# Attention and gated feed-forward layer: six one-bank PSUM tiles in place of three two-bank tiles

## The chip, the cores and the metric

The kernel runs on one core of one Trainium2 chip. The core has five engines, each with its own instruction stream: TensorE (PE; its weight loads are listed as PEld), VectorE (DVE), ScalarE (ACT), GpSimd (POOL) and SyncE (SP), which issues the DMAs here. Matmul results go to PSUM, an accumulator memory that this kernel uses in banks of 512 float32 values per partition. Engines wait for one another through semaphores. The metric is the time of one execution on the device in microseconds (us).

## The reference

```python
def _attn_ref(q, k, v, n_sink, window):            # B 4, H 8, S 768, D 64
    scores = (1.0 / np.sqrt(D)) * np.matmul(q, k.transpose(0, 1, 3, 2))
    pos = np.arange(S)
    rel = pos[:, None] - pos[None, :]
    keep = (pos[None, :] < n_sink) | ((rel >= 0) & (rel < window))   # 4 and 128
    scores = np.where(keep, scores, -1e9)
    a = np.exp(scores - scores.max(-1, keepdims=True))
    a = a / (a.sum(-1, keepdims=True) + 1e-9)
    return np.matmul(a, v)

def reference(...):
    x = attn_out.transpose(0, 2, 1, 3).reshape(B * S, H * D)          # 3072 x 512
    h = x @ w_in                                                      # 512 x 2048
    g = h - np.tanh(h)
    return (g @ w_out).astype(np.float32)                             # 2048 x 512
```

## The kernel before, in words

The 3072 rows of x are cut into 12 chunks of 256 (NCHUNK). Attention works in units of one chunk and one pair of heads, 48 in all; each unit has two blocks of 128 queries (t = 0, 1). The feed-forward part works in steps of one chunk (cc) and one of 8 weight groups (g) of 256 hidden columns, 96 in all. To keep float32 accuracy, operands are split into a high and a low part and multiplied in several passes.

**A unit.** `scores` multiplies a query block with a window of keys (L504 with raw operands for the first 12 units, L511 with split ones later); the two heads' results go to the two banks of one PSUM tile. `merge` works on that tile on VectorE: where `kind > 0`, L525 copies the earlier window's scores into the places that the later one leaves free, for both heads in one instruction, and then, head by head, L531 applies the mask and takes the row's extreme (an instruction and a short read of its accumulator). ScalarE takes the exponential (L539), VectorE the reciprocal of the sums (L559, L560), ScalarE scales (L565). `turn` transposes the probabilities into tbank (L599); from there ScalarE copies (L606, L616) and VectorE copies under a mask (L613). `attend` transposes the four sink columns into xbank (L640), ScalarE copies them out once per head of a pair (zr, L647), and L656 and L662 multiply with the values into xbank; ScalarE rounds the result (xh, L674) and VectorE takes the rest (xl, L678).

**A step.** L777 makes h in one of two h banks; ScalarE takes tanh (L796), VectorE the difference (L799), ScalarE the high part (L802), VectorE the low part (L805). The second product goes to an output bank by L847; from chunk 5 on (SA) a seven-product scheme is used instead (L881), whose sums lie in sbank and obank, with more vector work in the gate (L812, L815, L818). At the end of such a chunk `gather` takes the sums out: ScalarE copies the first bank of sbank (L920), VectorE adds the second bank of obank (L924), the second of sbank (L927, L929) and the first of obank (L933).

**Which bank holds what.** PSUM has eight banks, two for h and six in three tiles of two banks each:

```python
248  sbank = ps.tile([P, 2, 512], F32, tag="s", name="sbank")
249  obank = ps.tile([P, 2, 512], F32, tag="o", name="obank")
250  txbank = ps.tile([P, 2, 512], F32, tag="tx", name="txbank")
251  tbank, xbank = txbank[:, 0, :], txbank[:, 1, :]
```

Scores go to sbank up to chunk 5 and to txbank behind it; in the first units the second block goes to obank.

**What sets the order.** Nothing is issued as the loops run. Every piece of work is handed to `Work.add` with its engine, an estimated duration, a due time and what it reads and writes; here the six banks are six names (s0, s1, o0, o1, t, x). `Work.order` (L194 to L230) plays the estimates through and gives one list, by which each engine's instructions are recorded. The due times come from a few constants (L274 to L277): PACE is the time of a step, LEAD how far attention runs ahead of the steps that need it, HALF2 how far the second product follows the first, SPILL and STREAM the due times of two kinds of DMA. Behind this list, the layer that records the program puts in the semaphore waits; it knows tiles.

**Stages.** The steps of chunks 0 to 2 are interleaved while the weights are still coming in, are decoded to high and low parts on the chip, and are written to a scratch memory (spill, `wscr`). From step 24 on, the first weights are read back from there through a ring of five blocks (`ring`, `spare`); the place in SBUF that comes free takes sums of weights for the seven-product scheme (L985, L987, L989 on `wide`, then L1001 to L1008).

## Time and profile before

| what | value |
|---|---|
| median of 3 runs | 714.76 us (714.32 to 716.55) |
| profiled execution | 713.8 us |
| its span in the trace | 712.0 us |
| mean granted TensorE clock | 0.993 of full speed |
| busy: PE, PEld | 666.9 us, 611.2 us |
| busy: DVE, ACT, POOL | 551.4, 410.0, 177.2 us |
| DMA | 137.23 MB, HBM 191 GB/s over the span |

The rows come from the profiled execution alone. A busy time counts when at least one instruction of the engine ran; "[1.00 <-DVE wide L929]" says that the engine stood idle for 1.00 us before this instruction and that VectorE's L929, which writes `wide`, was what ended the wait. Such releasers are inferred. Matmuls of one line are drawn together as x4 and the like.

### The profile page before, as it was taken

Reading aid. Unit: us, or ns where it says so; the run is one execution under the profiler, and the core shown is the slowest. Engines: PE = TensorE matmul, PEld = TensorE weight load, DVE = VectorE, ACT = ScalarE, POOL = GpSimd, SP = SyncE. Lnnn points to the kernel's source line nnn. Section 1 sums busy time; section 2 is a strip of 40 time slices with the busy share of each in tenths; the row PEclk is TensorE's granted clock in tenths of the full one; section 3 lists DMA queues with packets and bytes.
Section 4 is the critical chain, followed back from the end, with each engine's and each line's share of the span. In section 5 each row is a group of like instructions: output and inputs, shape, how many; then the busy total and the mean of one; then the engine's idle time right before and its main releaser. Section 6 shows DMA issues by size and latency. Waiting matters only on the chain.

```text
span 712.0 us, 14370 instructions
## 1 busy us (share of the span) xinstructions
PE 666.9 (94%) x5099; PEld 611.2 (86%) x5099; DVE 551.4 (77%) x1305; ACT 410.0 (58%) x1056; POOL 177.2 (25%) x287
## 2 busy tenths in 40 slices
PE   6788999999999997999999999999999998999896
PEld 5556899889988787889889889999999998999895
DVE  6777998964878898889878768877886876875554
ACT  5876333345876675656567557566565665663231
POOL 5332100001436464313222212223111231210000
PEclk9999999999999998999999999999999999999999
DMA  6769972432148665657857865866775775664761
GB/s 187 244 198 335 351 293 104 152 115 86 53 116 242 187 194 155 194 161 232 229 178 200 258 185 174 239 211 190 232 220 185 210 239 167 180 184 135 237 192 65
DMA packets 77485, 137.23 MB, mean 193 GB/s; under 512 B 8156, under 2 KB 28764, under 8 KB 77404
## 3 DMA queue, kind: packets, MB, share of 16 engines
q1 hardware_dynamic: 77404, 136.22, 62.0%
q8 instruction: 42, 0.69, 0.4%
q14 instruction: 39, 0.32, 0.1%
HBM read 120.98 MB, written 15.20 MB: 191 GB/s over the span
## 4 chain that ended last, share of the span: by engine, by line
PE 71%; DVE 10%; DMA 7%; ACT 6%; issue 2%; POOL 1%; SPq 0%; ACTq 0%; DVEq 0%
PE h L777 30%; PE sbank L881 10%; PE obank L881 7%; DMA ring<-wscr 6%; PE txbank L662 5%; PE obank L847 5%; PE txbank L847 3%; PE sbank L847 3%; PE txbank L511 3%; PE txbank L599 2%; DVE pt L613 2%; PE sbank L511 1%; ACT p L565 1%; PE txbank L656 1%; ACT pt L616 1%
## 5 line engine op out<-in xcount | busy, mean ns | idle before, releaser
L777 PE MATMUL h<-xh,ring 128*128 128x256 f32 x924 | 185.8, 282 | 8.6 <-DMA ring<-wscr 5.5
L777 PEld LDWEIGHTS h<-xh,ring 128*128 128x128 f32 x924 | 151.3, 190 | 10.9 <-DMA ring<-wscr 7.0
L777 PE MATMUL h<-xl,ring 128*128 128x256 f32 x462 | 129.0, 279 | 0.0
L796 ACT ACTIVATE gbuf<-h 128x512 f32<-128x512 f32 x96 | 57.3, 597 | 105.5 <-PE h L777 65.8
L482 POOL TENSOR_TENSOR q<-qraw,q 128x512 fp32r<-128x512 f32 x36 | 47.4, 1318 | 254.5 <-ACT q L479 254.5
L777 PEld LDWEIGHTS h<-xl,ring 128*128 128x128 f32 x462 | 87.6, 190 | 0.4
L539 ACT ACTIVATE p<-p,st 128x132 f32<-128x132 f32 x168 | 66.5, 398 | 26.8 <-DVE st L531 25.6
L815 ACT CAST ghbuf<-gbuf 128x896 fp32r<-128x896 f32 x55 | 51.9, 943 | 39.1 <-DVE gbuf L812 38.7
L777 PE MATMUL h<-xh,w 128*128 128x256 f32 x384 | 73.4, 281 | 0.0
L818 DVE TENSOR_TENSOR glbuf<-gbuf,ghbuf 128x896 fp32r<-128x896 f32 x55 | 61.2, 1112 | 15.2 <-ACT ghbuf L815 13.6
L777 PEld LDWEIGHTS h<-xh,w 128*128 128x128 f32 x384 | 60.8, 188 | 1.3 <-PE txbank L662 0.2
L565 ACT ACTIVATE p<-p,st 128x132 f32<-128x132 f32 x168 | 54.2, 394 | 4.3 <-DVE st L560 3.8
L474 DVE TENSOR_TENSOR ks<-kraw,ks 64x392 fp32r<-64x392 f32 x72 | 49.5, 687 | 5.6 <-ACT ks L469 3.0
L777 PE MATMUL h<-xl,w 128*128 128x256 f32 x192 | 53.5, 279 | 0.0
L847 PE MATMUL obank<-w,ghbuf 128*128 128x512 f32 x192 | 51.5, 399 | 1.4 <-ACT ghbuf L802 1.4
L799 DVE TENSOR_TENSOR gbuf<-h,gbuf 128x512 f32<-128x512 f32 x55 | 37.9, 689 | 18.8 <-ACT gbuf L796 18.3
L777 PE MATMUL h<-xh,spare 128*128 128x256 f32 x228 | 50.7, 285 | 0.2 <-DMA spare<-wscr 0.2
L619 POOL TENSOR_TENSOR pt<-pt,after 128x512 f32<-128x512 f32 x32 | 43.4, 1358 | 29.4 <-ACT pt L616 27.3
L613 DVE TENSOR_TENSOR pt<-txbank,below 128x512 f32<-128x512 f32 (+1 forms) x48 | 28.9, 602 | 26.8 <-ACT pt L616 9.7
L574 POOL CAST z<-p 128x16 fp32r<-128x16 f32 x42 | 11.5, 274 | 124.4 <-ACT p L565 119.2
L662 PE MATMUL txbank<-pt,v 128*64 128x128 f32 (+1 forms) x512 | 41.5, 315 | 0.0
L662 PEld LDWEIGHTS txbank<-pt,v 128*64 128x64 f32 x512 | 31.0, 137 | 11.8 <-issue 4.6
(157 smaller groups left out, 1620.8 us busy)
## 6 DMA issues: line engine op xcount, KB each, us to landing
ring<-wscr SPq DMA_DIRECT2D x231, 256.0 KB, 4.1
spare<-wscr SPq DMA_DIRECT2D x57, 256.0 KB, 4.1
qraw<-qd SPq DMA_DIRECT2D x36, 256.0 KB, 4.6
wraw<-w_in SPq DMA_DIRECT2D x16, 512.0 KB, 8.2
wraw<-w_out SPq DMA_DIRECT2D x16, 512.0 KB, 8.2
wscr<-w SPq DMA_DIRECT2D x16, 512.0 KB, 4.9
kraw<-kp SPq DMA_DIRECT2D x38, 196.0 KB, 3.9
v<-vp SPq DMA_DIRECT2D x27, 256.0 KB, 2.9
```

What stands on the lines that cost most here:

```text
L474: (nc.gpsimd if KP else nc.vector).tensor_tensor(k[o, h, :], t[r, :], k[r, h, :].bitcast(F32), op=ALU.subtract)
L482: (nc.gpsimd if QP else nc.vector).tensor_tensor(ql[u], qt[u], qh[u].bitcast(F32), op=ALU.subtract)
L539: nc.scalar.activation(e, e, AF.Exp, bias=st[u][:, j : j + 1], scale=-1.0, accum_out=st[u][:, 4 + j : 5 + j],)
L565: nc.scalar.activation(pr[u][:, j, :], pr[u][:, j, :], AF.Copy, scale=s[:, 8 + j : 9 + j])
L619: nc.gpsimd.tensor_tensor(w[:, :, 0, :], w[:, :, 0, :], after.unsqueeze(1).to_broadcast([P, 4, P]), op=ALU.mult)
L662: nc.tensor.matmul(xps[key][(p - p0) // 2][h * 64 : h * 64 + 64, p % 2, a:z], lhsT=vt[cc, i][:, hd : hd + D], rhs=rhs, start=False, stop=p ...
L777: nc.tensor.matmul(hps[n][:, f, :], lhsT=w, rhs=x, start=r == 0, stop=r == 11)
L796: nc.scalar.activation(g0, h(), AF.Tanh)
L815: nc.scalar.copy(ghbuf[:, n % 2], gbuf[:, 1:, :])
L818: nc.vector.tensor_tensor(glbuf[:, :7, :], gbuf[:, 1:, :], ghbuf[:, n % 2].bitcast(F32), op=ALU.subtract)
L847: nc.tensor.matmul(sums_of(n, cc, t), lhsT=a[:, f, t * P : (t + 1) * P], rhs=wt[1, g][:, (0, 1, 0)[i], f, :], start=first and not low and ...
L881: nc.tensor.matmul(acc, lhsT=a[:, b, :], rhs=factor(g, m, part % 2), start=g == 0 and part == 0 and m in (4, 1, 2, 7), stop=closes(n) and ...
```

## The change

Each of the six banks becomes a tile of its own; sbank, obank and txbank become pairs of tiles. Since an instruction can no longer span the two heads' banks, the masked merge L525 is issued for each head by itself, right ahead of that head's mask instruction. Of 80 such merges 160 become. Five constants of the planner have other values. The change shortens the file by five lines: L525 is L524 in the new kernel, L531 L526, L613 L608, L777 L772, L799 L794, L805 L800, L881 L876. TensorE and ScalarE keep their instructions (5516 and 1080 in the program), VectorE has 1819 in place of 1739.

```diff
-        sbank = ps.tile([P, 2, 512], F32, tag="s", name="sbank")
-        obank = ps.tile([P, 2, 512], F32, tag="o", name="obank")
-        txbank = ps.tile([P, 2, 512], F32, tag="tx", name="txbank")
-        tbank, xbank = txbank[:, 0, :], txbank[:, 1, :]
+        banks = {n: ps.tile([P, 512], F32, tag=n, name=n) for n in ("s0", "s1", "o0", "o1", "t", "x")}
+        sbank, obank, txbank = ((banks[a], banks[b]) for a, b in (("s0", "s1"), ("o0", "o1"), ("t", "x")))
+        tbank, xbank = txbank
...
-        FIRST, EARLY, PACE, LEAD = 45000.0, 4600.0, 7980.0, 43356.0
+        FIRST, EARLY, PACE, LEAD = 45000.0, 4600.0, 7956.0, 43418.0
         UNIT, SECOND, WLEAD, WNEXT = 2000.0, 3000.0, 6000.0, 2500.0
-        HALF2, LAST = 8253.0, 6188.0
-        SPILL, STREAM, DEAR, DLATE = 36773.0, 5446.0, 120000.0, 17426.0
+        HALF2, LAST = 9148.0, 6188.0
+        SPILL, STREAM, DEAR, DLATE = 47526.0, 10850.0, 120000.0, 17426.0
...
                 both = obank if apart else sbank if cc <= SA else txbank
-                ps = [both[:, h, :] for h in range(2)]
-                sps[u, t] = both, ps
+                ps = sps[u, t] = both
...
-                both, ps = sps[u, t]
+                ps = sps[u, t]
...
-                if kind > 0:
-                    nc.vector.copy_predicated(
-                        both[:, :, TS:WIN], above.bitcast(U32).unsqueeze(1).to_broadcast([P, 2, P]),
-                        both[:, :, :P],
-                    )
                 for h in range(2):
+                    if kind > 0:
+                        nc.vector.copy_predicated(ps[h][:, TS:WIN], above.bitcast(U32), ps[h][:, :P])
                     j = 2 * h + t
                     nc.vector.tensor_tensor_reduce(
...
-            4: (sbank[:, 0, :HALF], 1), 3: (sbank[:, 0, HALF:], 0), 1: (obank[:, 1, :HALF], 2),
+            4: (sbank[0][:, :HALF], 1), 3: (sbank[0][:, HALF:], 0), 1: (obank[1][:, :HALF], 2),
```

The other lines of the diff only write `bank[:, i, ...]` as `bank[i][:, ...]`.

The merges of the first units on VectorE (p and st are the probabilities and sums of one unit) before:

```order
L525 COPY_PREDICATED obank<-above,obank 128x2x128 [waits PE_49]
L531 ISA p_292,st_293<-obank,mask 128x132 [waits DVE_49]
L531 ISA st_293 128x1
L531 ISA p_292,st_293<-obank,mask 128x132
L531 ISA st_293 128x1
```

And now, where o_238 and o_239 are the two banks of obank:

```order
L524 COPY_PREDICATED o_238<-above,o_238 128x128 [waits PE_49]
L526 ISA p_296,st_297<-o_238,mask 128x132 [waits DVE_49]
L526 ISA st_297 128x1
L524 COPY_PREDICATED o_239<-above,o_239 128x128 [waits PE_49]
L526 ISA p_296,st_297<-o_239,mask 128x132 [waits DVE_49]
L526 ISA st_297 128x1
```

One merge over both heads has become two, each ahead of its head's mask, and each mask waits for its own merge.

TensorE at the end of chunk 5, where the first L881 of the next chunk follow (edge and w_0 are weights of the seven-product scheme, ghbuf the high part of the gate) before:

```order
L881 MATMUL sbank<-edge_2480,ghbuf 128x256 [waits DVE_49,Activation_49]
L881 MATMUL sbank<-edge_2480,ghbuf 128x256 x3
L881 MATMUL obank<-edge_2480,ghbuf 128x256 x2
L777 MATMUL h_4463<-xh_4114,spare 128x256 [waits DMAHW3_49,PE_49]
L777 MATMUL h_4463<-xl_4115,spare 128x256
L777 MATMUL h_4463<-xh_4114,spare 128x256 x2
L777 MATMUL h_4463<-xl_4115,spare 128x256
L777 MATMUL h_4463<-xh_4114,spare 128x256
L881 MATMUL sbank<-w_0_764,ghbuf 128x256 x4
```

And now, with s_236 and s_237 the banks of sbank and o_239 the second bank of obank:

```order
L876 MATMUL s_236<-edge_2502,ghbuf 128x256 [waits Activation_49]
L876 MATMUL s_236<-edge_2502,ghbuf 128x256 x3
L876 MATMUL o_239<-edge_2502,ghbuf 128x256 [waits DVE_49]
L876 MATMUL o_239<-edge_2502,ghbuf 128x256
L772 MATMUL h_4514<-xh_4161,spare 128x256 [waits DMAHW3_49,PE_49]
L772 MATMUL h_4514<-xl_4162,spare 128x256
L772 MATMUL h_4514<-xh_4161,spare 128x256 x2
L772 MATMUL h_4514<-xl_4162,spare 128x256
L772 MATMUL h_4514<-xh_4161,spare 128x256
L876 MATMUL s_237<-w_0_778,ghbuf 128x256 [waits DVE_49]
L876 MATMUL s_237<-w_0_778,ghbuf 128x256 x3
```

The order is the same. The first L881 waited for VectorE and ScalarE and now waits for ScalarE alone; waits for VectorE stand at the first matmul on o_239 and at the first on s_237.

VectorE around the gate of step 29 (h_2658 is that step's h), where the difference L799 of that step stands three rows above the first row; before:

```order
L985 TENSOR_TENSOR wide<-w_4_1318 128x512 [waits DVE_49]
L987 TENSOR_TENSOR wide<-wide,w_4_1318 128x512 [waits DVE_49]
L678 TENSOR_TENSOR xl_2765<-txbank,xh_2764 128x512 [waits PE_49,Activation_49]
L678 TENSOR_TENSOR xl_2765<-txbank,xh_2764 128x512
L525 COPY_PREDICATED sbank<-above,sbank 128x2x128 [waits PE_49]
L531 ISA p_2703,st_2704<-sbank,mask 128x132 [waits DVE_49]
L531 ISA st_2704 128x1
L531 ISA p_2703,st_2704<-sbank,mask 128x132
L531 ISA st_2704 128x1
L805 TENSOR_TENSOR glbuf<-h_2658,ghbuf 128x512
L447 SCALAR_TENSOR_TENSOR vsink<-vsink,sides,vraw 64x128 [waits Activation_49,Pool_49]
L447 SCALAR_TENSOR_TENSOR vsink<-vsink,sides,vraw 64x128 [waits Activation_49]
```

And now (h_2697 is the same step's h, L794 the old L799 and L800 the old L805):

```order
L524 COPY_PREDICATED s_237<-above,s_237 128x128 [waits PE_49]
L526 ISA p_2726,st_2727<-s_237,mask 128x132 [waits DVE_49]
L526 ISA st_2727 128x1
L794 TENSOR_TENSOR h_2697<-h_2697,gbuf 128x512 [waits Activation_49]
L982 TENSOR_TENSOR wide<-wide,w_4_1333 128x512
L984 TENSOR_TENSOR wide<-wide,w_4_1333 128x512 [waits DVE_49]
L446 SCALAR_TENSOR_TENSOR vsink<-vsink,sides,vraw 64x128 [waits Pool_49]
L446 SCALAR_TENSOR_TENSOR vsink<-vsink,sides,vraw 64x128
L554 TENSOR_SCALAR st_2727<-st_2727 128x4 [waits Activation_49]
L555 RECIPROCAL st_2727<-st_2727 128x4 [waits DVE_49]
L800 TENSOR_TENSOR glbuf<-h_2697,ghbuf 128x512 [waits Activation_49]
```

The difference of step 29 has moved behind the unit's second merge, and with it the low part, which now follows two sums of weights and the reciprocal. Moves of this kind, a gate instruction or a group of scores against its neighbours, are found for steps 23 to 29 and units 17 to 20; 22 matmuls of TensorE and 5 instructions of ScalarE move, none of GpSimd's. On SP the first spills, `wscr<-w_0`, stand behind eight loads of keys, queries and weights ahead of which they stood.

## Rows read from the trace of the kernel before

**Rows 1.** The page, busy time of each engine, its share of the span and the instructions.

```profile
PE 666.9 (94%) x5099; PEld 611.2 (86%) x5099; DVE 551.4 (77%) x1305; ACT 410.0 (58%) x1056; POOL 177.2 (25%) x287
```

**Rows 2.** Windows of the span by stage: the stretch, its length, then the busy time (and instructions) of PE, PEld, DVE, ACT and POOL, the granted TensorE clock, the DMA share and GB/s.

```profile
0.00:57.00 57.00, 43.33 (x240) 31.90 (x240) 40.83 (x179) 41.33 (x155) 22.51 (x68) 1.00 0.70 218
...
85.00:166.00 81.00, 81.00 (x523) 73.08 (x522) 65.81 (x77) 30.79 (x46) 1.29 (x1) 1.00 0.47 173
...
200.00:285.00 85.00, 78.68 (x550) 69.08 (x550) 74.47 (x166) 55.52 (x155) 46.02 (x58) 0.96 0.63 182
285.00:350.00 65.00, 64.44 (x466) 58.21 (x465) 56.12 (x134) 42.59 (x115) 18.18 (x25) 1.00 0.68 201
350.00:660.00 310.00, 297.62 (x2584) 286.60 (x2582) 236.81 (x591) 186.31 (x458) 70.06 (x107) 1.00 0.67 200
```

**Rows 3.** TensorE's waits between 0 and 85 us: line and tile of the waiting instruction, what ended the wait, us in total, times, the longest.

```profile
PE txbank L599 <- ACT zr L647: 3.9, 3, 1.6
...
PE txbank L656 <- DVE pt L613: 2.5, 2, 1.3
PE sbank L504 <- DVE obank L525: 1.7, 1, 1.7
PE txbank L599 <- DVE xl L678: 1.5, 3, 0.5
PE txbank L640 <- ACT pt L606: 1.0, 1, 1.0
PE txbank L599 <- ACT xh L674: 0.8, 1, 0.8
```

**Rows 4.** The same view from 85 us to the end.

```profile
PE h L777 <- DMA ring<-wscr: 5.5, 7, 1.8
PE sbank L881 <- DVE wide L929: 4.4, 5, 1.0
...
PE txbank L640 <- DVE pt L613: 2.4, 4, 1.0
...
PE obank L847 <- ACT ghbuf L802: 1.4, 1, 1.4
PE txbank L640 <- ACT pt L616: 1.0, 1, 1.0
...
PE sbank L881 <- ACT wide L920: 0.7, 2, 0.3
```

**Rows 5.** The timeline of all engines between 27 and 31 us: start, duration, engine, line, operation, and in brackets the idle time before it and its releaser.

```profile
28.12 0.37 ACT L606 COPY pt<-txbank 128x256 f32<-128x256 f32 x1 [1.23 <-PE txbank L640]
...
28.39 0.48 ACT L647 ACTIVATE zr<-txbank,sides 128x256 fp32r<-128x256 f32 x1
...
28.90 0.43 DVE L613 TENSOR_TENSOR pt<-txbank,below 128x256 f32<-128x256 f32 x1 [0.92 <-ACT zr L647]
29.36 0.47 ACT L647 ACTIVATE zr<-txbank,sides 128x256 fp32r<-128x256 f32 x1 [0.49 <-DVE pt L613]
...
29.87 0.42 DVE L613 TENSOR_TENSOR pt<-txbank,after 128x256 f32<-128x256 f32 x1 [0.54 <-ACT zr L647]
...
30.35 0.49 PE L656 MATMUL txbank<-zr,vsink 128*128 128x512 f32 x1 [1.17 <-DVE pt L613]
```

**Rows 6.** The timeline of TensorE between 394 and 398 us, at the end of a chunk.

```profile
395.57 0.71 PE L881 MATMUL sbank<-edge,ghbuf 128*128 128x256 f32 x4 [1.00 <-DVE wide L929]
396.11 0.40 PE L881 MATMUL obank<-edge,ghbuf 128*128 128x256 f32 x2
...
397.06 0.63 PE L881 MATMUL sbank<-w,ghbuf 128*128 128x256 f32 x4
```

**Rows 7.** The timeline of VectorE between 261 and 263 us, one merge with its masks and the instruction behind.

```profile
261.39 0.42 DVE L525 COPY_PREDICATED sbank<-above,sbank 128x256 f32<-128x256 uint32 x1
261.84 0.29 DVE L531 CUSTOM_DVE_ANT_0 p<-sbank,mask 128x132 f32<-128x132 f32 x1
...
262.06 0.29 DVE L531 CUSTOM_DVE_ANT_0 p<-sbank,mask 128x132 f32<-128x132 f32 x1
...
262.27 0.69 DVE L805 TENSOR_TENSOR glbuf<-h,ghbuf 128x512 fp32r<-128x512 f32 x1
```

**Rows 8.** Groups of instructions with shapes kept apart, the two forms of L613: busy us in total, mean ns of one, idle time before and its releasers.

```profile
L613 DVE TENSOR_TENSOR pt<-txbank,below 128x512 f32<-128x512 f32 x32 | 22.1, 691 | 19.1 <-ACT pt L616 9.7 <-PE txbank L599 6.6 <-PE txbank L640 2.8
...
L613 DVE TENSOR_TENSOR pt<-txbank,below 128x256 f32<-128x256 f32 x16 | 6.8, 423 | 7.7 <-ACT xh L674 3.0 <-ACT zr L647 2.1 <-ACT pt L606 1.1
```

**Rows 9.** L525 alone by stage: the stretch, its length, busy time and count on VectorE, granted clock, DMA share, GB/s.

```profile
0.00:85.00 85.00, 4.97 (x12) 1.00 0.77 256
...
200.00:285.00 85.00, 5.16 (x13) 0.96 0.63 182
...
350.00:660.00 310.00, 16.11 (x38) 1.00 0.67 200
```

**Rows 10.** The timeline of all engines at 280 us, and behind the dots the window of 280 to 285 us in the columns of rows 2.

```profile
280.31 0.68 DVE L805 TENSOR_TENSOR glbuf<-h,ghbuf 128x512 fp32r<-128x512 f32 x1
...
281.09 0.55 PE L777 MATMUL h<-xh,ring 128*128 128x256 f32 x1 [3.14 <-issue]
...
280.00:285.00 5.00, 3.91 (x18) 3.94 (x19) 3.56 (x12) 3.35 (x10) 0.00 (x0) 0.50 0.21 48
```

More of the change, by code (lines that the diff above doesn't have):

```diff
@@ L836, in sums_of @@
         def sums_of(n, cc, t):
-            return (sbank, txbank, obank)[{1: 0, 2: 1, NCHUNK - 1: 1}.get(cc, 2)][:, t, :]
+            return (sbank, txbank, obank)[{1: 0, 2: 1, NCHUNK - 1: 1}.get(cc, 2)][t]
         def mm2(n, k):
@@ L855, in _banded @@
         accs = {
-            4: (sbank[:, 0, :HALF], 1), 3: (sbank[:, 0, HALF:], 0), 1: (obank[:, 1, :HALF], 2),
-            2: (sbank[:, 1, :HALF], 3), 5: (sbank[:, 1, HALF:], 4),
-            7: (obank[:, 0, :HALF], 6), 6: (obank[:, 0, HALF:], 5),
+            4: (sbank[0][:, :HALF], 1), 3: (sbank[0][:, HALF:], 0), 1: (obank[1][:, :HALF], 2),
+            2: (sbank[1][:, :HALF], 3), 5: (sbank[1][:, HALF:], 4),
+            7: (obank[0][:, :HALF], 6), 6: (obank[0][:, HALF:], 5),
         }
@@ L919, in copy @@
             def copy():
-                nc.scalar.copy(v, pair(sbank[:, 0, :]))
+                nc.scalar.copy(v, pair(sbank[0][:, :]))
             def add1():
-                one = obank[:, 1, :HALF].unsqueeze(1).to_broadcast([P, 2, HALF])
+                one = obank[1][:, :HALF].unsqueeze(1).to_broadcast([P, 2, HALF])
                 nc.vector.tensor_tensor(u, one, v, op=ALU.add)
             def add2():
-                nc.vector.tensor_tensor(v, pair(sbank[:, 1, :]), v, op=ALU.add)
+                nc.vector.tensor_tensor(v, pair(sbank[1][:, :]), v, op=ALU.add)
                 for k in range(2):
-                    nc.vector.tensor_tensor(u[:, k, :], u[:, k, :], sbank[:, 1, (1 - k) * HALF : (2 - k) * HALF], op=ALU.subtract)
+                    nc.vector.tensor_tensor(u[:, k, :], u[:, k, :], sbank[1][:, (1 - k) * HALF : (2 - k) * HALF], op=ALU.subtract)
             def add3():
                 for k in (1, 0):
-                    nc.vector.tensor_tensor(u[:, k, :], obank[:, 0, k * HALF : (k + 1) * HALF], u[:, k, :], op=ALU.add)
+                    nc.vector.tensor_tensor(u[:, k, :], obank[0][:, k * HALF : (k + 1) * HALF], u[:, k, :], op=ALU.add)
             def put(t):
@@ L952, in add4 @@
                 part = four[:, 0::3, :] if t else four[:, 1:3, :]
-                nc.vector.tensor_tensor(part, pair(txbank[:, t, :]), part, op=ALU.add)
+                nc.vector.tensor_tensor(part, pair(txbank[t][:, :]), part, op=ALU.add)
             def end():
```

## The prediction, before the result was known

> **What bounds the kernel now.** I read the shares of the page first: TensorE is busy 666.9 of 712.0 us, VectorE 551.4 [rows 1]. So no more than 45 us can go while TensorE's work stays, and the change leaves that work alone. Then the windows by stage [rows 2]. From 85 to 166 us TensorE is busy in every microsecond; whatever the start gains before 85 is therefore carried on unless the weights come late. Before 57 it is busy 43.33 of 57, with ScalarE at 41.33 and VectorE at 40.83: three engines that hand small pieces to each other, a latency stage. From 200 to 285 VectorE is at 74.47 of 85 (88%) and TensorE loses 6.3 us: VectorE sets the pace there. From 350 to 660 TensorE is at 297.6 of 310 and VectorE has 73 us to spare.
>
> Next, what TensorE waited for, before 85 us [rows 3] and behind it [rows 4]. The reader should ask of each row which bank is written and which bank the one waited for reads. The transposes of L599 write t; zr (L647), xl (L678) and xh (L674) read x. L656 starts with x and waited for L613, which reads t. L640 writes x and waited for L606, L616 and L613, which read t. L881 starts a new chunk in the first bank of sbank and waited for L929, which reads the second. So 9.7 us before 85 (all of [rows 3] but the 1.7: there L504 writes sbank and the releaser read obank, another tile, so that this wait is no neighbour's and stays) and 8.5 us behind it ended with a neighbour's bank, not with the instruction's own.
>
> The timeline shows the pattern at work [rows 5]: ScalarE copies t, VectorE's L613 on t starts only when zr has read x, the second zr starts only when L613 has read t, the second L613 waits for that zr. Four steps in a row, of which only zr after zr and L613 after L613 have anything to do with each other. A dependency kept for the whole two-bank tile explains all of it; with six tiles these edges are not made.
>
> **The change, part by part.** The sum is made against the profiled execution: 713.8 us, of which 712.0 are the span. The median of the runs shown is 714.76, 1.0 higher.
>
> *The waits that go, start.* Where a wait goes, the next late thing decides.
> - L599 behind zr, 3.9 in three: behind two of them ScalarE's copy of t ends right before the two zr's, which last 0.48 and 0.47 [rows 5]; so 0.95 each, and the third (3.9 - 2 x 1.6 = 0.7) whole: 2.6.
> - L656 behind L613, 2.5 in two: zr is next. In [rows 5] the second zr could start at 28.9 and end near 29.35, so L656 starts about 1.0 before its 30.35: 2.0.
> - L599 behind xl 1.5 and xh 0.8: its probabilities were there long before; whole, 2.3.
> - L640 behind L606, 1.0: xl, which reads x, is next and ends inside the gap; half, 0.5.
>
> That is 7.4. Other work fills part of what comes free: VectorE and ScalarE are busy some 41 of 57 us, and loads arrive when they arrive. Bounds: nothing if these two take up every gap, 9.7 if none does. Nearest to the rows is that they fill the same share as they fill now (0.72 each), but they also overlap each other; I keep two thirds, 4.9.
>
> *The waits that go, later* [rows 4]. At a chunk's end TensorE stood 1.0 us before L881 [rows 6]; L929 reads the second bank, which is touched only by the L881 at 397.06, 1.5 us behind, when L929 is over; the copy out of the first bank, L920, is first in the gather. So all five, 4.4, and the two behind L920, 0.7. L640: 2.4 + 1.0. Sum 8.5. Next late is the ring of weight blocks, on which TensorE already waits 5.5 us in seven places; a block that is freed earlier is fetched earlier only by as much. Bounds: 8.5 if the ring has slack, 3.0 if the ring takes another 5.5. I give back a third: 5.7.
>
> *The merges.* 80 merges of 2x128 become 160 of 128. One group takes from L525 at 261.39 to the next instruction at 262.27, 0.88 us [rows 7]. The halved form is in no row. L613 gives the shape's price: 512 columns 691 ns, 256 columns 423 [rows 8], so 1.05 ns a column and 155 ns fixed. A merge of 256 at 0.42 fits; one of 128 is then 0.29, and a group with two of them with the start of the next instruction 0.03 behind each is 0.32 + 0.22 + 0.32 + 0.22 = 1.08: 0.20 more. Bounds: 0.0 if it is columns alone, 0.45 if half a merge costs what a whole one does. I take 0.20, by the two forms of L613; 80 x 0.20 = 16 us of VectorE. What of it is seen depends on the stage [rows 9]: 12 before 85 (2.4 us; half, since the finer merge also starts one head earlier: 1.2), 13 from 200 to 285 (2.6; VectorE sets the pace but waits 10.5 us there itself: half, 1.3), 38 from 350 to 660 (7.6 against 73 us of idle VectorE: 0.5). The cover in that last stage is the TensorE work of the step, behind which VectorE's gate already finishes; if it is gone the whole 7.6 is due.
>
> The Trainium skill, "VectorE: DVE Perf Modes", section "The DRAIN you can't avoid", speaks against this part: it says that each Vector instruction pays its flush whatever one does, that a semaphore between two costs nothing extra, and so that instructions are to be saved, not semaphores. By that rule alone the change trades what is free for what is dear, and its time would be that of the slower rival below. The 155 ns fixed in [rows 8] bear the first half out; the 18 us of TensorE's waits in [rows 3, 4] are not of the kind the page speaks of, since they lie between engines.
>
> *The order.* The planner's numbers move little: on TensorE score and transpose groups of units 17 to 20 and one six-matmul block of step 29, on VectorE L799 and L805 of steps 24 to 29 around them, on SP the spills of the first weights behind eight loads. All lies between 200 and 285 us or is queue order. Price 0, bounds 1.4 either way (one wait of the size of the largest that a high part of the gate, L802, brings in [rows 4] would come or go). What is queued behind the later L805 of step 29 on VectorE is a score merge, and L805 itself is waited for by the low products of that step and by the first half of step 31; both stand several matmul blocks later in TensorE's order. On SP the spills of the first weights are passed by eight loads of keys, queries and weights; these issue earlier and nothing reads the spilled blocks before the ring starts behind step 23.
>
> Sum: -4.9 + 1.2 - 5.7 + 1.3 + 0.5 = -7.6; 713.8 - 7.6 = 706.2, on the median's level 707.2. Between the two I say 706.5.
>
> **The rivals.**
> 1. *Everything goes.* If the removed waits go whole and the merges hide: 713.8 - 9.7 - 8.5 = 695.6. For it: 85 to 166 carries anything. Against it: [rows 5] show chains whose next link is close by. With half of the merges' visible 3.0 us and ring waits some 699.
> 2. *The gaps only change their name.* VectorE and ScalarE hold the start, the ring holds the end: 4.9 shrinks to 1.5, 5.7 to 3.0, the merges cost 3.0: 713.8 - 1.5 = 712.3. For it: the ring's seven waits. Against it: the chunk ends lie outside the ring's waits.
> 3. *Slower: VectorE falls behind between 200 and 285.* At 277.95 TensorE stood 3.14 us; the row names no releaser, but L805, which reads the h bank that a later step writes again, ends at 280.99, 0.1 before the matmul. TensorE then ran at a granted clock of 0.50, that is 1.2 instead of 2.4 GHz, from 280 to 285 [rows 10]; 3.91 busy us there are worth half, so 2.0 more. If the 13 merges (2.6) bring one more such stop (3.1 + 2.0), the start's 12 merges (2.4) are paid whole and VectorE eats the start's gain, it is 713.8 + 2.6 + 5.1 + 2.4 - 5.7 = 718.2. It decides from where VectorE's own waits in that stretch, 10.5 us now, no longer lie between two merges. For it: 88% busy. Against it: the merges there lie ahead of such waits, not in the run of additions that makes the stop.
> 4. *It does nothing.* If dependencies were kept by bank already, only the merges stay: 713.8 + 3.0 = 716.8. [rows 5] speak against it.
>
> **How the numbers follow.** Likeliest case 0.68, from 702 to 710 by its own bounds; rival 1 0.12; rival 2 0.11; rival 3 0.07; rival 4 0.02. About 0.3% (2.1 us) is what a measurement here can tell from no change, so faster is below 712.6: the first two cases and a quarter of rival 2, 0.83; same 0.08; slower 0.09. The range of 700 to 713 leaves out rivals 3 and 4 and about half of rival 1.
>
> **What would show it.** Right: TensorE's waits on zr, xl, xh and L613 before 85 nearly gone and the first full stretch of TensorE reached 3 to 5 us earlier; L881 at chunk ends without L929; L525 160 times at about 0.29; ring waits up from 5.5 to some 8; the stop at 281 still there. Wrong: L525 above 0.35; a second stretch with the clock at half; waits on L613 or L531 in place of the old ones before 57; the 85 to 166 stretch no longer full, which would mean the weights hold the start.

## The result and the profile after

The changed kernel takes 695.78 us (median of four runs, 694.41 to 697.55) against 714.54 us before; the ratio is 0.9734, with a 95% interval of 0.9701 to 0.9768. It is 18.8 us faster: the direction was forecast, the size was not (706.5, with 700 to 713 as the range). The value is that of the first rival, "everything goes", to 0.2 us. The profiled execution took 696.93 us, its span is 695.2 us.

Busy times on the page of the changed kernel, to be set beside [rows 1]:

```profile
PE 663.2 (95%) x5099; PEld 609.7 (88%) x5099; DVE 565.3 (81%) x1385; ACT 411.5 (59%) x1056; POOL 175.9 (25%) x287
```

VectorE works 13.9 us more; besides it only ScalarE's time grew, by 1.5. The windows, with bounds moved by hand to the stages' new places; columns as in [rows 2]:

```profile
0.00:52.00 52.00, 43.23 (x250) 32.51 (x251) 42.19 (x193) 41.40 (x157) 23.84 (x68) 1.00 0.73 233
...
78.00:155.00 77.00, 77.00 (x502) 69.68 (x501) 64.31 (x75) 29.58 (x44) 1.29 (x1) 1.00 0.49 171
...
188.00:275.00 87.00, 80.13 (x563) 68.98 (x562) 79.19 (x185) 56.72 (x160) 45.74 (x61) 0.99 0.61 181
275.00:340.00 65.00, 65.00 (x469) 59.27 (x469) 57.52 (x145) 45.41 (x121) 17.32 (x24) 0.99 0.67 202
340.00:645.00 305.00, 298.12 (x2600) 288.39 (x2599) 246.95 (x632) 188.06 (x460) 70.07 (x108) 1.00 0.68 204
```

The start does the same 43 us of TensorE work in 52 us instead of 57, and the stretch that TensorE fills begins earlier and is full again. To say where the rest came from, I mark each step by the start of its first matmul: L777 (now L772) runs 24 times a step, so step n begins with the (24n + 1)st. From those marks, in us:

| stretch | before | after | difference |
|---|---|---|---|
| start to step 2 | 70.17 | 62.65 | -7.52 |
| steps 2 to 20 | 102.76 | 102.68 | -0.08 |
| steps 20 to 37 | 133.13 | 132.02 | -1.11 |
| steps 37 to 49 | 82.25 | 80.01 | -2.24 |
| steps 49 to 95 | 307.83 | 302.69 | -5.14 |
| step 95 to the end | 15.90 | 15.12 | -0.78 |

The last column adds up to 16.9, not 18.8: the marks compare one profiled execution of each kernel (713.84 and 696.93 us), the 18.8 is of medians. A second profiled execution of the changed kernel (694.63 us, from the run beside merges ahead, below) has 62.74, 102.68, 131.04, 80.78, 300.43 and 15.12 in the same six stretches. Two executions of one kernel thus differ by 2.3 us between steps 49 and 95, and a smaller difference of marks there says little by itself.

TensorE's waits up to 80 us, which answer to [rows 3] (line and tile of the waiting instruction, what ended the wait, total, times, longest):

```profile
PE s L502 <- DVE o L524: 2.1, 1, 2.1
PE t L594 <- ACT pt L601: 1.4, 3, 0.6
...
PE x L635 <- DVE xl L673: 0.5, 1, 0.5
```

The waits of the transposes on zr, xl and xh are gone; L594 now waits for the copy of its own bank. Behind 80 us, to be set beside [rows 4]:

```profile
PE h L772 <- DMA ring<-wscr: 5.0, 6, 1.5
PE h L772 <- issue: 3.1, 1, 3.1
...
PE s L876 <- ACT ghbuf L810: 1.4, 3, 0.5
PE h L772 <- DMA spare<-wscr: 1.3, 1, 1.3
```

L881's waits on L929 and L920 and L640's on L613 and L616 are gone. New is a short one, the first second-half matmul on the gate's high part (L810). The waits for the ring and `spare` together are 6.3 us where they were 5.7; the prediction had looked for some 8. The chain of [rows 5], some units later in the changed kernel, all engines (start, duration, engine, line, operation):

```profile
23.85 0.36 ACT L601 COPY pt<-t 128x256 f32<-128x256 f32 x1
...
24.22 0.59 ACT L669 CAST xh<-x 128x512 fp32r<-128x512 f32 x1
24.25 0.42 DVE L608 TENSOR_TENSOR pt<-t,below 128x256 f32<-128x256 f32 x1
...
24.59 0.41 DVE L608 TENSOR_TENSOR pt<-t,after 128x256 f32<-128x256 f32 x1
```

VectorE's two L608 read t while ScalarE reads x, side by side, 0.34 us from one to the next instead of 0.97. The end of chunk 5 on TensorE, [rows 6] in the new kernel:

```profile
383.22 0.40 PE L509 MATMUL x<-ks,q 128*128 128x260 f32 x2
383.46 0.63 PE L876 MATMUL s<-edge,ghbuf 128*128 128x256 f32 x4
```

No stop. The gain is more than the row of 1.00 had said: step 49 took 8.04 us and takes 6.81, 1.23 less. Before, L511's last matmul ended at 394.57 and L881 began at 395.57; now L876 begins 0.16 before L509's end, since a matmul here begins before the one in front has come to its end (its drain), and its four take 0.63 in place of 0.71. Together these are 0.24, where the gain beyond the row is 0.23. At all five chunk ends together it is 1.23 + 1.19 + 1.28 + 1.10 + 1.13 = 5.9 us where the rows had 4.4.

The merge, [rows 7] in the new kernel on VectorE:

```profile
413.60 0.29 DVE L524 COPY_PREDICATED t<-above,t 128x128 f32<-128x128 uint32 x1 [0.20 <-PE t L509]
414.03 0.30 DVE L526 CUSTOM_DVE_ANT_0 p<-t,mask 128x132 f32<-128x132 f32 x1
...
414.25 0.29 DVE L524 COPY_PREDICATED x<-above,x 128x128 f32<-128x128 uint32 x1
414.58 0.29 DVE L526 CUSTOM_DVE_ANT_0 p<-x,mask 128x132 f32<-128x132 f32 x1
```

A half merge lasts 0.29, as worked out from [rows 8]. The stop that rival 3 spoke of is there as before ([rows 10]):

```profile
272.93 0.68 DVE L800 TENSOR_TENSOR glbuf<-h,ghbuf 128x512 fp32r<-128x512 f32 x1
...
273.72 0.55 PE L772 MATMUL h<-xh,ring 128*128 128x256 f32 x1 [3.13 <-issue]
```

### The profile page after: what moved, and what is told of

The parts are those of the page before. It is cut to its first block, busy times and chain, and to the rows that moved or that the text cites. A ratio compares the mean times of both kernels' runs of the same rounds, so it can differ in the third digit from the quotient of the medians.

```text
span 695.2 us, 14415 instructions
## 1 busy us (share of the span) xinstructions
PE 663.2 (95%) x5099; PEld 609.7 (88%) x5099; DVE 565.3 (81%) x1385; ACT 411.5 (59%) x1056; POOL 175.9 (25%) x287
## 4 chain that ended last, share of the span: by engine, by line
PE 71%; DVE 14%; ACT 6%; DMA 5%; issue 2%; POOL 1%; SPq 0%; DVEq 0%; POOLq 0%; ACTq 0%
PE h L772 29%; PE s L876 10%; PE o L876 7%; PE o L842 6%; PE s L842 3%; PE x L657 3%; DMA ring<-wscr 3%; PE t L594 2%; PE t L657 2%; PE t L842 2%; PE x L842 2%; PE t L509 1%; PE x L509 1%; DVE wide L982 1%; PE s L509 1%
## 5 line engine op out<-in xcount | busy, mean ns | idle before, releaser
L772 PE MATMUL h<-xh,ring 128*128 128x256 f32 x924 | 185.4, 282 | 8.2 <-DMA ring<-wscr 5.0
L772 PEld LDWEIGHTS h<-xh,ring 128*128 128x128 f32 x924 | 150.9, 189 | 10.4 <-DMA ring<-wscr 6.3
L772 PE MATMUL h<-xl,ring 128*128 128x256 f32 x462 | 128.8, 279 | 0.0
L772 PEld LDWEIGHTS h<-xl,ring 128*128 128x128 f32 x462 | 87.4, 189 | 0.3
L810 ACT CAST ghbuf<-gbuf 128x896 fp32r<-128x896 f32 x55 | 51.8, 943 | 41.4 <-DVE gbuf L807 41.2
L813 DVE TENSOR_TENSOR glbuf<-gbuf,ghbuf 128x896 fp32r<-128x896 f32 x55 | 62.0, 1128 | 14.7 <-ACT ghbuf L810 10.7
L772 PE MATMUL h<-xh,w 128*128 128x256 f32 x384 | 73.4, 281 | 0.0
L772 PEld LDWEIGHTS h<-xh,w 128*128 128x128 f32 x384 | 60.8, 188 | 1.3 <-PE x L657 0.2
L794 DVE TENSOR_TENSOR gbuf<-h,gbuf 128x512 f32<-128x512 f32 x55 | 37.9, 689 | 19.4 <-ACT gbuf L791 18.9
L772 PE MATMUL h<-xl,w 128*128 128x256 f32 x192 | 53.5, 279 | 0.0
L842 PE MATMUL o<-w,ghbuf 128*128 128x512 f32 x192 | 51.5, 399 | 1.3 <-ACT ghbuf L797 1.3
L772 PE MATMUL h<-xh,spare 128*128 128x256 f32 x228 | 50.6, 285 | 1.3 <-DMA spare<-wscr 1.3
L608 DVE TENSOR_TENSOR pt<-t,below 128x512 f32<-128x512 f32 (+1 forms) x48 | 28.9, 601 | 19.5 <-ACT pt L611 7.9
L772 PEld LDWEIGHTS h<-xh,spare 128*128 128x128 f32 x228 | 39.0, 189 | 1.8 <-DMA spare<-wscr 1.5
L842 PEld LDWEIGHTS o<-w,ghbuf 128*128 128x128 f32 x192 | 33.6, 188 | 7.2 <-ACT ghbuf L797 1.5
```

Of the source, the lines that this page charges most:

```text
L772: nc.tensor.matmul(hps[n][:, f, :], lhsT=w, rhs=x, start=r == 0, stop=r == 11)
L794: nc.vector.tensor_tensor(g0 if strassen(n) else h(), h(), g0, op=ALU.subtract)
L810: nc.scalar.copy(ghbuf[:, n % 2], gbuf[:, 1:, :])
L813: nc.vector.tensor_tensor(glbuf[:, :7, :], gbuf[:, 1:, :], ghbuf[:, n % 2].bitcast(F32), op=ALU.subtract)
L842: nc.tensor.matmul(sums_of(n, cc, t), lhsT=a[:, f, t * P : (t + 1) * P], rhs=wt[1, g][:, (0, 1, 0)[i], f, :], start=first and not low and ...
```

## The experiments

Theory A says that waits between neighbouring banks are the gain. The rivals are the planner's numbers (B) and the finer merges (C). Fourteen kernels ran; each ratio is to runs of the kernel before on the same chip.

**The two parts, and the banks by pairs.** First the six tiles with the old numbers:

```diff
-        FIRST, EARLY, PACE, LEAD = 45000.0, 4600.0, 7956.0, 43418.0
+        FIRST, EARLY, PACE, LEAD = 45000.0, 4600.0, 7980.0, 43356.0
...
-        HALF2, LAST = 9148.0, 6188.0
-        SPILL, STREAM, DEAR, DLATE = 47526.0, 10850.0, 120000.0, 17426.0
+        HALF2, LAST = 8253.0, 6188.0
+        SPILL, STREAM, DEAR, DLATE = 36773.0, 5446.0, 120000.0, 17426.0
```

> Six tiles and merges by head, but the planner's five numbers as before, so that every engine keeps the order of before. Theory A (the waits on a neighbour's bank are the whole gain, the numbers are worth under 1.5 us): 695 to 698, step 2 begins 7.0 to 7.6 us earlier than before, and L881's waits on L929 are gone. Rival B (the numbers carry a third or more of the 18.8 us): 701 to 708, with the missing part in the stretch of steps 20 to 40, where the order moves.

Measured: 698.23 us against 713.68, ratio 0.978 (0.974 to 0.982); step 2 begins 7.4 us ahead. The same lines the other way round in the kernel before:

> The three two-bank tiles and the merges over both heads of before, with the five new numbers alone. Theory A: within 2 us of before, 713 to 716. Rival B: 706 to 711. If the new numbers are only good with the new tiles, they may also cost: 716 to 718.

Measured: 715.74, ratio 1.0016 (0.9997 to 1.0035). The numbers do nothing that can be told from nothing, with either tiles (0.978 with the old ones, 0.9734 and, measured again below, 0.976 with the new): B falls. Then only txbank as two tiles:

```diff
-        txbank = ps.tile([P, 2, 512], F32, tag="tx", name="txbank")
-        tbank, xbank = txbank[:, 0, :], txbank[:, 1, :]
+        txbank = tuple(ps.tile([P, 512], F32, tag=n, name=n) for n in ("t", "x"))
+        tbank, xbank = txbank
```

> Old numbers; only txbank becomes two tiles (t and x), sbank and obank stay two-bank tiles with merges over both heads; scores that lie in txbank (chunks 6 to 11) are merged by head. Theory A, by banks: the start's waits all lie between t and x, so step 2 begins about 7.5 us earlier, and the later waits of L640 and L511 on L613 and L616 (some 4.5 us) go as well: 702 to 704. Waits of L881 on L929 and L920 (5.1) stay. Rival C (the merges by head, not the banks, bring the start forward): step 2 begins less than 3 us earlier, 708 to 711.

And only sbank and obank as two each:

```diff
-        banks = {n: ps.tile([P, 512], F32, tag=n, name=n) for n in ("s0", "s1", "o0", "o1", "t", "x")}
+        banks = {n: ps.tile([P, 512], F32, tag=n, name=n) for n in ("s0", "s1", "o0", "o1")}
+        tx = ps.tile([P, 2, 512], F32, tag="tx", name="txbank")
+        banks["t"], banks["x"] = tx[:, 0, :], tx[:, 1, :]
```

> Old numbers; sbank and obank become two tiles each, txbank stays one, all merges by head. Theory A: L881's waits on L929 and L920 go (5.1 idle, some 6 with the pipeline that runs on), the start's waits stay, step 2 begins within 1 us of before: 707 to 710. Rival C: step 2 begins 4 us earlier or more, 704 or less. If the two parts add up, this one's gain and that of the split of txbank alone sum to the gain of six tiles with old numbers within 2 us.

Measured: txbank alone 700.19, ratio 0.9817 (0.9787 to 0.9848), step 2 begins 8.1 us ahead; the other two alone 713.51, ratio 1.0002 (0.9976 to 1.0029), step 2 2.0 us behind. (In that profile the granted clock between 40 and 46 us is 0.72, where the kernel before has 1.00, so that the 2.0 say nothing of the tiles.) The start is txbank's, as A had it, and C falls there. The two gains, 13.5 and 0.2 us, add up to 13.7 where six tiles with the old numbers gain 15.5, within the 2 us expected; but how they divide was not foreseen: the second kernel gains nothing, where A had 707 to 710. TensorE's waits of it from 85 us on (L637 is L640 of the kernel before, L610 its L613, L528 its L531):

```profile
PE txbank L637 <- DVE pt L610: 2.3, 4, 0.9
PE txbank L511 <- DVE pt L610: 1.3, 1, 1.3
...
PE txbank L511 <- DVE st L528: 0.7, 2, 0.4
```

L929 is gone from this list, so the five chunk ends were gained; something took them back, and the list has no new wait large enough for that.

**What the merges cost.** The kernel before with nothing but merges by head:

```diff
-                if kind > 0:
-                    nc.vector.copy_predicated(
-                        both[:, :, TS:WIN], above.bitcast(U32).unsqueeze(1).to_broadcast([P, 2, P]),
-                        both[:, :, :P],
-                    )
                 for h in range(2):
+                    if kind > 0:
+                        nc.vector.copy_predicated(ps[h][:, TS:WIN], above.bitcast(U32), ps[h][:, :P])
```

> The three two-bank tiles and the numbers of before; only the merge is done by head, 160 of 128 columns in place of 80 of 2x128. Every wait between neighbouring banks stays. By the trace of the changed kernel these merges are 12.5 us more of VectorE work (46.3 against 33.8). Theory A (little of it is seen; the gain is the tiles'): 714.5 to 717, that is 1 to 3 us above before, no gain anywhere. Rival C (finer merges by themselves bring the start forward): 708 or less.

Measured: 720.47 against 715.53, ratio 1.0077 (1.0052 to 1.0102): 4.9 us lost, more than the 1 to 3 that A had; C falls altogether. By the marks 4.1 of them lie between steps 49 and 95 (311.95 against 307.83), 1.1 before step 2 and 1.0 between steps 20 and 37 (134.09 against 133.13). That would account for the split of sbank and obank: it too merges by head in an undivided txbank between steps 49 and 95, 5.9 gained and 4.1 lost leave 1.8, and its marks show 1.6 (306.21). The sum fits, but that it is the merges which took the gain back in that kernel is argued from it and not shown by a run of its own. Then each merge of the changed kernel twice:

```diff
-                        nc.vector.copy_predicated(ps[h][:, TS:WIN], above.bitcast(U32), ps[h][:, :P])
+                        for _ in range(2):
+                            nc.vector.copy_predicated(ps[h][:, TS:WIN], above.bitcast(U32), ps[h][:, :P])
```

> The changed kernel with each of its 160 merges issued twice in a row (the second copies the same scores again), some 46 us more on VectorE: 7 before 52 us, 5 between 155 and 188, 7.5 between 188 and 275, 5 between 275 and 340, 22 behind. If merges are hidden wherever VectorE waits: 698 to 703, with the loss in the start and between 188 and 275 alone. If half of each merge is seen, as the prediction had it in the stretches before 85 and from 200 to 285: 704 to 710. A merge then also delays the mask behind it, so the start loses 3 to 6 us.

Measured: 730.83, ratio 1.0221 (1.019 to 1.0253). That is far outside both expectations: 35 us for 46 us of merges. Its marks put 20.3 of them between steps 49 and 95 (323.02 against 302.69), the stretch where the prediction had 73 us of VectorE to spare. TensorE's waits from 85 us on say why (this file is one line longer there: L877, L814 and L811 are L876, L813 and L810 of the changed kernel):

```profile
PE s L877 <- DVE glbuf L814: 6.1, 8, 1.1
PE s L877 <- ACT ghbuf L811: 4.9, 8, 1.1
...
PE x L509 <- DVE st L527: 2.5, 8, 0.4
```

The gate's high and low parts come late: a step's gate has VectorE in its chain, and idle time elsewhere in the step doesn't cover what is put into it.

**Which property of the merges costs.** The changed kernel with both merges ahead of both masks:

```diff
-                for h in range(2):
-                    if kind > 0:
-                        nc.vector.copy_predicated(ps[h][:, TS:WIN], above.bitcast(U32), ps[h][:, :P])
+                for h in range(2 if kind > 0 else 0):
+                    nc.vector.copy_predicated(ps[h][:, TS:WIN], above.bitcast(U32), ps[h][:, :P])
+                for h in range(2):
```

Beside it the changed kernel again:

> The changed kernel itself once more, beside the three that follow: 694 to 698. Its start is measured a second time: step 2 begins 6.5 to 8.5 us ahead of the profile of before, if the start's gain is of the tiles and not of one lucky execution.

> The changed kernel with both heads' merges ahead of both masks, as before the change; the same 160 merges. The first bank is then read to its end 0.3 us later. Theory F (behind chunk 5 the dearer merges cost nothing because each head's bank is given back by itself, merge and mask in one go): scores of t = 1 come late by up to 0.3 us in some 20 units, and the start too, 1 to 5 us slower than the changed kernel. Rival G (the place of the merge doesn't matter, there is room in any case): within 1 us of it.

Measured: the changed kernel 697.27, ratio 0.976 (0.9732 to 0.9789), step 2 7.4 us ahead once more; merges ahead 693.21, ratio 0.9685 (0.9655 to 0.9716). Both F and G were wrong: it is 4.1 us faster, and beats both kernels. The two profiled executions don't show the whole of it (their spans are 692.8 and 693.2 us): the granted clock between 18 and 25 us is 1.00 in the changed kernel's and 0.76 in that of merges ahead, whose step 2 begins 2.1 us later. Its VectorE at the place shown above:

```profile
414.93 0.30 DVE L523 COPY_PREDICATED t<-above,t 128x128 f32<-128x128 uint32 x1 [0.24 <-PE t L509]
415.17 0.30 DVE L523 COPY_PREDICATED x<-above,x 128x128 f32<-128x128 uint32 x1
415.38 0.29 DVE L526 CUSTOM_DVE_ANT_0 p<-t,mask 128x132 f32<-128x132 f32 x1
...
415.59 0.29 DVE L526 CUSTOM_DVE_ANT_0 p<-x,mask 128x132 f32<-128x132 f32 x1
...
415.81 0.69 DVE L794 TENSOR_TENSOR gbuf<-h,gbuf 128x512 f32<-128x512 f32 x1
```

From the first merge to L794 it is 0.88 us, as with one merge in [rows 7]; in the changed kernel it was 1.20 (413.60 to 414.80). The durations are the same. An instruction that needs nothing of the one in front begins 0.21 to 0.24 behind it, before that one's end; a mask behind its own merge begins 0.33 to 0.43 behind. Over the 26 to 43 groups of a kernel whose instructions follow one another without idle time, the medians from the first merge to the instruction behind are 0.89 before, 1.09 after and 0.87 here. The mask still waits for its own merge; that merge is now two instructions in front of it and no longer one. TensorE's waits from 80 us on have lost L876 on L810, which came three times in both profiles of the changed kernel (1.4 us in all in either):

```profile
PE h L772 <- DMA ring<-wscr: 4.5, 5, 1.4
PE h L772 <- issue: 3.1, 1, 3.1
PE s L509 <- DVE ks L473: 1.6, 3, 0.8
```

Does order alone do it, without new tiles? The same diff in the kernel before:

> The kernel before with its three tiles and numbers; 160 merges by head, both of a pair ahead of both masks. Theory H (a mask right behind the merge of its own bank starts only when that has ended and a little more, 0.33 to 0.43 us from start to start, while instructions that don't depend on the last one follow after 0.21 to 0.24; so the order within the pair costs, not the number of instructions): a group takes 0.88 us from the first merge to the instruction behind, as with one merge over both heads, and the time is within 2 us of before, 713 to 716. Rival I (each further VectorE instruction costs its fixed part, as the prediction had it): as the kernel with merge and mask in turn, 718 to 721.

Measured: 719.54, ratio 1.0064 (1.0037 to 1.0091), what rival I had said. But its VectorE shows a wait, not a count:

```profile
284.83 0.62 DVE L525 COPY_PREDICATED sbank<-above,sbank 128x128 f32<-128x128 uint32 x2
285.48 0.30 DVE L528 CUSTOM_DVE_ANT_0 p<-sbank,mask 128x132 f32<-128x132 f32 x1
...
285.70 0.29 DVE L528 CUSTOM_DVE_ANT_0 p<-sbank,mask 128x132 f32<-128x132 f32 x1
...
285.92 0.69 DVE L796 TENSOR_TENSOR h<-h,gbuf 128x512 f32<-128x512 f32 x1
```

Two merges take 0.62 together, one behind the other, because they write one tile; I had overlooked that. In the order of the program the second has a wait on VectorE's own semaphore here and none in six tiles:

```
L525 COPY_PREDICATED sbank<-above,sbank 128x128 [waits PE_49]
L525 COPY_PREDICATED sbank<-above,sbank 128x128 [waits DVE_49]

L523 COPY_PREDICATED o_238<-above,o_238 128x128 [waits PE_49]
L523 COPY_PREDICATED o_239<-above,o_239 128x128 [waits PE_49]
```

So H holds as to the mechanism (with the same 160 instructions a group is 1.09 or more where a mask or a merge waits for the one right in front of it, and 0.87 where it doesn't), and my expectation of this kernel failed since the false dependency is one between VectorE's own instructions too.

**What is given back at the ring.** Two kernels with a ring of half the bytes, in six tiles and with only txbank split, old numbers in both. The first product takes each block's first half twice:

```diff
-            nc.sync.dma_start(ring[i].bitcast(F32), wscr[g][:, j * WG // 2 : (j + 1) * WG // 2])
+            nc.sync.dma_start(ring[i][:, : WG // 4].bitcast(F32), wscr[g][:, j * WG // 2 : j * WG // 2 + WG // 4])
...
-                w = block[:, d % 2, a, :]
+                w = block[:, 0, a, :]
```

> Six tiles with the old numbers, and a ring of half the bytes: each block's load brings only its first 256 columns, and the first product takes these twice in place of the second 256 (other results, the same matmuls). To be set against the next kernel, which has the same ring and only txbank split. Theory D (what the chunk ends gain is given back at the ring's loads): without the ring's waits this kernel keeps all of it, some 5 us ahead of the next one between steps 49 and 95, where with whole loads it was 2.5. Rival E (it is given back at the gate behind VectorE's gather, waits of L876 on L810): still some 2.5 ahead, and returned steps 75 and 83 look as before. Either way 690 to 695.

> Only txbank split, old numbers, and the same ring of half the bytes as the kernel before this one. The ring's waits (some 4.6 us in the run with whole loads) go, L886's waits on L934 (4.4) stay: 694 to 698. Theory D: 3 to 4 us slower than six tiles with this ring. Rival E: within 2 us of it.

Measured: 691.75, ratio 0.9668 (0.9646 to 0.9689), and 695.47, ratio 0.9731 (0.9708 to 0.9753): 3.7 us apart, 4.7 between steps 49 and 95 (297.33 against 302.07). With whole loads the medians are 2.0 apart and the marks 2.5 (303.45 against 305.96). The numbers are those of D; but the 1.7 us by which the two pairs of medians differ are within the scatter of four runs each, so that the ring takes back a part of the chunk ends is not shown.

E's part, the gate, is. In the first profile of the changed kernel five steps became longer than before by more than 0.5 behind step 49: 67 by 1.12 and 72 by 0.79, where TensorE waits for `spare` or the ring, and 59, 75 and 83 by 0.80, 0.84 and 0.81, where L876 waits for L810. In its second profile 59, 75 and 83 are longer by 0.81, 0.84 and 0.81 again, but 67 and 72 by 0.29 and 0.17 alone, and the waits for the ring and `spare` have come down from 6.3 to 4.8 us:

```profile
PE h L772 <- DMA ring<-wscr: 4.3, 6, 1.8
...
PE s L876 <- ACT ghbuf L810: 1.4, 3, 0.5
...
PE h L772 <- DMA spare<-wscr: 0.5, 1, 0.5
```

With the short ring 67 and 72 are shorter than before (5.52 against 5.97, 7.10 against 7.34) and 75 and 83 stay long; with merges ahead of masks 59, 75 and 83 are within 0.03 of before, in that kernel and in the last one below. So what is late at the ring changes from one execution to the next, while what is late at these three gates, 2.5 us, comes with the order of merge and mask.

**The stop in front of step 34.** On VectorE the low part of one step's gate, or those of steps 24 to 39, directly behind their last prerequisite:

```diff
         todo, _ = work.order()
+        for n in (32,):
+            todo.remove(lows[n])
+            todo.insert(1 + max(todo.index(a) for a in work.all[lows[n]][4]), lows[n])
```

> The changed kernel, and on VectorE the low part of the gate of step 32 is put ahead of what the planner had set before it (two differences of keys and three sums of weights). In the changed kernel's trace it could have begun at 268.0 and began at 272.9, and TensorE stood 3.1 us until it ended and then ran 3.4 us at half clock. If the stop hangs on that order: the 3.1 go, and with them the half clock, 1.7: 691 to 693. If the next link is as late (the ring's block, the keys' difference that is now 0.7 later): 0 to 2 us faster, 694 to 696.

> The changed kernel with the low part of the gate of every step from 24 to 39 put directly behind its last prerequisite in the recorded order; five of them move on VectorE, step 32's among them. As the kernel before this one, 690 to 693, if VectorE's sums of weights can all wait; slower than it by 1 to 3 us if the later sums then hold up the chunk that uses them first.

Measured: 696.37, ratio 0.9738 (0.9705 to 0.977), and 694.93, ratio 0.973 (0.9697 to 0.9764), against 0.976 for the changed kernel: the stop goes and little comes of it; 690 to 693 came for neither. In the first, the split of keys moved behind it is late instead, and the granted clock falls even so (0.72 between 270 and 276 us); TensorE's waits from 85 us on:

```profile
PE h L772 <- DMA ring<-wscr: 5.4, 6, 1.9
PE s L509 <- DVE ks L473: 2.3, 3, 1.0
PE t L509 <- DVE pt L608: 1.4, 1, 1.4
```

Merges ahead of masks and the low parts together:

> The changed kernel with both merges ahead of both masks and, in the order of the record, the low parts of the gates of steps 24 to 39 directly behind their last prerequisite. If the two gains (4 us and 2 us) add: 689 to 692. If the room that the first leaves on VectorE already lets the low part through in time: 692 to 694, and the stop of 3 us in front of step 34 tells which.

Measured: 691.28 against 715.35, ratio 0.9673 (0.9653 to 0.9693). Not to be told from merges ahead alone (0.9685) by the intervals; the window shows what the second edit did (columns as in [rows 2]):

```profile
200.00:285.00 85.00, 80.30 (x546) 70.08 (x545) 72.44 (x175) 53.69 (x149) 45.27 (x58) 1.00 0.64 195
```

The granted clock, 0.96 there in the kernel before and with merges ahead alone, is 1.00, with no stop of 3 us.

## Why the prediction was wrong

The mechanism was right: a dependency was kept for a whole two-bank tile, and 18.2 us of named waits hung on it. Two discounts in the sum failed, and a third term came near in total with its parts in the wrong places.

- *Start, "I keep two thirds, 4.9".* With its merges the sum had -3.7 here. Measured: -7.5, merges included, and -8.1 in the two kernels with only txbank split, whose first units merge over both heads. My own list of next late things had given 7.4; it was the sum, and the share for "other work fills part of what comes free" was put on top of a list that already had it. The other kernels with six tiles and merges in turn range from -6.3 to -7.9; the lowest of these had a granted clock of 0.76 between 18 and 25 us, the changed kernel 1.00.
- *Later, "I give back a third: 5.7".* With its merges the sum had -3.9 here. From step 20 on the marks show -8.5, and 0.8 more behind step 95: 9.3, and 11.7 in the second profile, merges included. The third was for the ring, and the ring did not take it: the waits for the ring and `spare`, 5.7 before, are 6.3 and 4.8 in the two profiles, not some 8. Also, what goes is larger than its rows: a stop costs the drain of the matmuls before it and the start of those behind as well (5.9 for rows of 4.4 at chunk ends; 1.17 and 1.23 at steps 45 and 53 for gaps of 1.02 and 1.00 before L640). The rows were read as the whole price; at these places they are its lower end.
- *Merges, +3.0.* The group was forecast at 1.08 and has a median of 1.09; the total, 4.1 by merges put ahead and 4.9 by merges alone, is near, though its parts are not. Merges alone lost 1.1 before step 2 and 1.0 between steps 20 and 37, for 1.2 and 1.3 in the sum; but "0.5 from 350 to 660, against 73 us of idle VectorE" was 4.1 between steps 49 and 95, and in the changed kernel 2.5, three gates each 0.8 late. Idle time of the stretch was taken for cover, and the gate's chain has none. The 17 merges left, between 166 and 200 and between 285 and 350, were put at nothing without a reason. The reason was wrong too: not the fixed part of an instruction but the wait on the one in front.
- *Order and numbers, 0.* No run speaks against it: 1.0016 alone; with six tiles 0.978 with the old numbers and 0.9734 and 0.976 with the new, intervals that overlap.
- *The rivals.* The first came to 0.2 us by luck, by numbers that cancel: its rows were too small (18.8 us of gain and 4.1 of merges make 22.9, its rows 18.2), and the merges were not in its 695.6. The second did not: the waits at the start went, with 1.4 us new on L594 (the old L599), and the ring's grew by no more than 0.6. The third did not: VectorE at 79 of 87 us from 188 to 275 makes the same single stop of 3.1. The fourth is excluded by the lists of waits.

The rule of the Trainium skill that I weighed ("VectorE: DVE Perf Modes", "The DRAIN you can't avoid": a semaphore between two Vector instructions costs nothing extra) does not hold for these short instructions: 160 merges, none with a mask of its own right behind it, make groups of 0.87 us, 80 whole ones 0.89, 160 with the mask waiting right behind its merge 1.09. The next section of the same page, "Two Vector instructions with no wait between them", says of instructions without a wait that a held one starts only when every earlier one has finished; one that isn't held, the first section adds, starts earlier. The starts 0.21 to 0.24 behind merges of 0.29 agree with that.

## What to carry to other kernels

Where one engine waits for another, compare the bank or slice that each touches, not the tile's name; if they differ, give each its own tile, and count such a stop at its row plus something (0.15 to 0.3 us each here). When an instruction is cut into pieces, put pieces that don't need each other next to each other. When a list of "what is late next" has been made, take its sum as the estimate: here a flat share on top of it was what went wrong. And profile a kernel twice before a difference of a microsecond or two between two traces is given a cause.

## What the runs showed of the hardware that I had not expected

VectorE's idle share says little about what it can take: merges by head in three tiles lengthened each of 80 groups by 0.32 us (medians of 1.21 and 0.89), 26 us, and cost 4.9; merges done twice were 46 us more and cost 35, with the engine at 609.4 of 729.3 us (84%) even then. And a dependency between neighbours on the same engine costs 0.1 us or more each time (0.33 against 0.21 from start to start), which no list of waits of another engine shows. Nor is the granted clock the same in every execution: between 18 and 25 us it is 1.00 in both profiles of the changed kernel and 0.76 with merges ahead and in the six tiles with the short ring, which begin step 2 between 1.2 and 2.2 us later.
